# Gathering the part-array products of a windowed-attention kernel into three places per half batch

## The chip, the core and the metric

The kernel runs on one core of one Trainium2 chip. The metric is the device time of one execution in microseconds (us). TensorE does the matrix products, VectorE and ScalarE the element-wise work, GpSimd (POOL) some constants and conversions, and the queues of SyncE and ScalarE start most DMA transfers.

## The reference

```python
def _attn_ref(q, k, v):                       # batch 4, 8 heads, 576 positions, 64 per head
    scores = (1 / np.sqrt(D)) * np.matmul(q, k.transpose(0, 1, 3, 2))
    rel = pos[:, None] - pos[None, :]
    mask_plain = (rel >= 0) & (rel < 32)                          # heads 0 to 3
    mask_dil = (rel >= 0) & (rel < 128) & (rel % 4 == 0)          # heads 4 to 7
    ...
    return np.matmul(attn, v)

def _moe_ref(x, w_in, w_out, alpha):          # 2304 tokens, 512 -> 2048 -> 512
    h = x @ w_in
    g = np.maximum(h, 0.0) + alpha * np.minimum(h, 0.0)
    return g @ w_out

def _moe2_ref(x, w_gate, w1, w2):             # 8 experts, 288 tokens each, 512 -> 1024 -> 512
    logits = x @ w_gate
    ...
    out[mask] = np.maximum(x[mask] @ w1[e], 0.0) @ w2[e]
```

`w_in` and `w_out` come as float64. The softmax goes over the allowed keys; the routing is greedy, highest logit first, until an expert has its 288 tokens. It compares logits, so they have to be exact to float32. The kernel computes the logits from the hidden layer `g` with `we = w_out @ w_gate`, ahead of the second product.

## The kernel before

Phase 1 (up to about 383 us of the profile) makes the attention and the hidden layer. A half batch (`hb`, 0 to 7) is 288 tokens. Its hidden layer is 16 chunks of 128 columns: `hid(hb, f)` is 12 products of the whole array (four parts of the model width, each as high by high, high by low and low by high), 288 columns each. The attention of a half batch is four pairs of heads (`n = 4 hb + pr`; `pr` 0 and 1 are undilated, 2 and 3 dilated).

A pair goes through these steps. `a_t` turns queries and keys (products with the identity), `a_te` takes them out of PSUM. `a_s` makes the scores of a pair: 64 rows of the array per head, so the two heads sit in two opposite quarters (`ps`; five tiles of 96 keys where undilated, four of 72 or 104 keys where dilated). `a_min` (the mask), `a_max`, `a_exp` and `a_norm` are the softmax. `a_pt` turns the weights, `a_pte` takes them out, `a_v` multiplies by the values: two heads side by side in the columns of the array (`po`). `a_vh` and `a_vl` split the result into the high and low part (`xh`, `xl`) that `hid` reads.

The gate logits of a quarter of the chunks are four products side by side, 32 columns of the array each (`logits`, tile `pl`). Half batches 0 to 3 get theirs later (`late`, tile `pll`), from `g` read back out of DRAM by `g_reload`. `l0_rows` turns finished logits into rows (`plt`). The 16 pieces of `w_out` are converted and give `we` by `wg_t`, `wg_m` (four products side by side, 32 columns each, tile `pw`) and `wg_s` (their sum, by a product with `sel`), with `wg_te`, `wg_me` and `wg_se` taking the results out of PSUM.

The order of the instructions is written by hand. Each step is put down with a place by `at(place, step)`; the unit is one chunk (`hid(hb, f)` is at 16 hb + f), and the list is sorted. Every engine works through its own instructions in that order. So the products that use a part of the array stand wherever the table puts them between two chunks: in the kernel before, `a_v` of pair n and `a_s` of pair n + 2 fall between the same two chunks, four times per half batch, and `logits`, `late` and `wg_m` have places of their own.

PSUM has three buffers for `pt`, `po`, `pll` and `plt` (tag `tp`), two for `ph`, one for scores, one for logits and gate weights (tag `lg`). Before chunk 0 the pieces of `w_in` come in over SyncE's queue and are converted by GpSimd, ScalarE and VectorE; the queue also brings queries, keys, values, `alpha` and `w_gate`. Phase 2 (`px`) is the second product with the routing beside it, phase 3 the experts; the change touches neither.

Of the kernel before, what the change touches and what calls it, by code (L numbers as in the profile page):

```python
# [7 lines left out]
F32 = mybir.dt.float32  # L8
# [12 lines left out]
# Places of the steps in the order of issue, in chunks of the hidden layer where they are fractions  # L21
# stages of the attention of a pair, from the first hidden chunk of its time
TA = dict(t=[-2.383, -1.666], te=[-2.203, -1.182], s=-0.544, min=-0.121, max=0.142, exp=[0.933, 2.385], norm=[1.571,
          3.182], pt=[4.914, 6.036], pte=[5.341, 6.32], v=7.254, vh=7.638, vl=7.784, lv=-1.319)
# shifts of the first eight pairs
NB = [2.769, 0.996, 0.321, -0.271, 0.257, 0.621, 0.11, -0.19]
# pairs whose scores get the mask by a product
PM = [0, 1, 2, 3, 4, 5, 6, 7]
# stages of the hidden layer and the gate logits
TH = dict(e=0.253, lg=1.298, lge=2.178, re=-2.126, late=2.001, latee=2.316)  # L30
# half batches whose gate logits come late
LATE = 4
# the late logits: first place, step
TL = [62.259, 2.506]
# pieces of w_in
WB = [-15.49, -15.159, -13.092, -12.092, -10.702, -9.556, -8.948, -5.584, -3.868, -3.649, -2.532, -1.004, -0.811,
      1.134, 3.634, 5.264]
# stages of a piece of w_in
TW = [-0.232, -0.154, 0.786, 1.291, 2.167, 2.365]
# first piece of w_out  # L40
W2 = 8.391
# step of the pieces of w_out
W3 = 3.139
# stages of a piece of w_out
TG = [-1.011, -0.417, 0.749, 1.085, 3.066, 3.243, 4.737, 5.74, 6.781, 6.86]
# end of the attention's buffers, after the last half batch began
TCLOSE = 0.814
# w_out again: loads, first split, step
TO = [-5.329, 3.863, 0.599]
# hidden layer read back: first load, step, first high and low parts  # L50
TGL = [-4.297, 1.335, -1.987, -1.486]
# second product: after which products the last logits and the routing start
XF = [1, 2]
# second product: hidden layer's load, high and low parts, by products modulo 4
GO = [0, 3, 3]
# second product: high and low parts of the first expert's weights
EO = [11, 11]
# time of those on the vector engine, ns
GC = 620
# start of the routing's chain, ns  # L60
RT0 = 3200
# how far it is issued ahead, ns
LEAD = 2000
# PSUM buffers of transposes
TP = 3
# PSUM buffers of long products
# [4 lines left out]
def window_attention_prelu_greedy_moe_kernel(  # L71
# [21 lines left out]
    W = 32                # window, in steps of a head's dilation  # L93
    R = 4                 # dilation of the upper half of the heads
    TQ = 72               # queries of a score tile
    TK = TQ + W           # keys that they can reach
    # undilated heads: queries of a tile (two heads side by side), their step, keys, tiles
    PQ, PS, PK, PT = 64, 56, 96, 5
    HB = S // 2           # tokens of a half batch
# [12 lines left out]
    ra = ctx.enter_context(pool("ra", 4))             # w_in, then experts 0, 2, ..  # L112
    ph_stg, ph_att = ExitStack(), ExitStack()
    stg = ph_stg.enter_context(pool("stg", 2))
    apool = ph_att.enter_context(pool("apool", 2, side="right"))
    ctx.enter_context(tc.manual_schedule())

    w_in, w_out = w_in.bitcast(I32), w_out.bitcast(I32)   # float64 as words (low, high)
# [11 lines left out]
    AT = {}  # L130

    def qk_rows(t, hp):
        # two heads side by side in each row of 128
        return t[:, 2 * hp:2 * hp + 2].rearrange("p h r d -> p (h r d)").rearrange("p (r h d) -> p r h d", r=R, h=2)

    def load_set(hb, s):
# [5 lines left out]
        for t, src in ((qt, q), (kt, k)):  # L142
            off = base + half * HB * D
            if hb == 0:
                # at the start as few transfers as can be
                nc.sync.dma_start(t.rearrange("p h r d -> p h (r d)"),
                                  dram_ap(src, off, [[R * D, TQ], [S * D, 4], [1, R * D]]))
                continue
# [5 lines left out]
    def load_v(hb, s):  # L154
        eng = nc.sync if hb == 0 else nc.scalar
# [3 lines left out]
        if s == 0:  # L159
            # tile t of the half: queries from 56 t, keys from 32 before  # L160
# [22 lines left out]
    # caps of the scores: -1e9 where a key is out of reach  # L183
    BIG = 3.0e38
    NEG = -1.0e9
    capp = apool.tile([P, PK], F32, name="capp", bufs=1)      # undilated: keys from 32 before: 1 <= kcol - q <= 32
    capp0 = apool.tile([P, PT, PK], F32, name="capp0", bufs=1)  # the same, its first tile without keys before 0
    capg = apool.tile([TQ, TK], F32, name="capg", bufs=1)     # dilated: keys from 32 before
    capd = apool.tile([TQ, TQ], F32, name="capd", bufs=1)     # keys from the tile's first: 0 <= q - kcol < 32

    def make_cap(dst, p0, lo, hi):
        # BIG where lo <= kcol - row <= hi, NEG elsewhere
# [14 lines left out]
    # the same caps to be added by a product: 0 in reach, -1e9 out of it  # L207
# [4 lines left out]
    def cap(n):  # L212
        # for a head, or for the two of a pair side by side
# [18 lines left out]
    wg = cpool.tile([P, ND, W], F32, name="wg")  # L232
    nc.gpsimd.memset(wg, 0.0)
# [101 lines left out]
    def wg_se(u):  # L335
        nc.vector.tensor_copy(we[:, u - NU, :], WP.pop(u))
# [889 lines left out]
```

## Time and profile before

| | |
|---|---|
| time, median of 3 runs (lowest to highest) | 863.08 us (863.08 to 863.16) |
| span of the profiled execution, first to last instruction | 859.0 us |
| time outside the span (863.08 - 859.0) | 4.1 us |
| TensorE busy | 823.5 us, 96% of the span |
| VectorE busy | 591.5 us, 69% |
| ScalarE busy | 425.3 us, 50% |

The profile is one execution. Matrix products are pipelined, so the duration of one says less than the distance from one start to the next: below, a block of products is "held" from its own first start to the first start of the next block. A row of a timeline joins equal neighbours (x16 is sixteen records; a float32 product is two records, a transpose one).

### The profile page before, as it was taken

The page shows a single profiled execution, that of the slowest core. Times are in us where ns is not written, and L with a number is a line of the kernel's source. Part 1 is how long each engine was busy: PE and PEld are TensorE (multiplying, and loading weights), DVE is VectorE, ACT ScalarE, POOL GpSimd, SP SyncE. Part 2 cuts the span into 40 slices and gives each one's busy share as a digit, 9 for nine tenths or more (in the row PEclk, how much of TensorE's full clock was granted, in tenths as well). Part 3 has the DMA queues.
Part 4 walks back from the last instruction along what each step waited for, and adds up shares of the span by engine and source line. Part 5 has one row for each costly group of instructions (what it writes and reads, how often), then busy time and mean ns, then how long its engine had stood idle before and what let it go on. Part 6 is the DMA issues. An engine that isn't in the chain of part 4 may idle for free.

```text
span 859.0 us, 17954 instructions
## 1 busy us (share of the span) xinstructions
PE 823.5 (96%) x6827; PEld 730.0 (85%) x6827; DVE 591.5 (69%) x1569; ACT 425.3 (50%) x1210; POOL 91.9 (11%) x138
## 2 busy tenths in 40 slices
PE   5689999999999999999999999999799999999996
PEld 4579999999888888887777777777599999999995
DVE  6899888777656556378888888888654455545630
ACT  4786565867565646482223322322045556555631
POOL 2531010100000000010000000000112212221111
PEclk9999999999999999999999999999889999999998
DMA  8856766654666762566434443334245667665600
GB/s 188 245 173 190 211 205 201 192 173 128 194 174 203 187 175 70 200 200 220 135 85 137 136 135 99 110 103 155 77 123 180 188 189 219 184 185 177 193 28 29
DMA packets 147179, 137.39 MB, mean 160 GB/s; under 512 B 56596, under 2 KB 122004, under 8 KB 147092
## 3 DMA queue, kind: packets, MB, share of 16 engines
q1 hardware_dynamic: 114700, 102.51, 39.8%
q10 hardware_dynamic: 29320, 24.29, 9.6%
q0 software_dynamic: 3072, 9.44, 3.7%
q8 instruction: 54, 0.88, 0.4%
q14 instruction: 33, 0.27, 0.1%
HBM read 103.70 MB, written 32.51 MB: 159 GB/s over the span
## 4 chain that ended last, share of the span: by engine, by line
PE 85%; issue 6%; DMA 3%; DVE 2%; POOL 2%; ACT 1%; SPq 1%; POOLq 0%; ACTq 0%; DVEq 0%
PE ph L124 33%; PE px L124 24%; PE py L124 9%; PE ps L124 3%; PE po L124 3%; PE pc L124 3%; PE pt L485 2%; PE pt L355 2%; PE pll L124 1%; PE pl L124 1%; PE pw L124 1%; POOL out_dram L1130 1%; DMA kt<-in_k_dram 1%; PE pt L316 1%; PE pty L1127 1%
## 5 line engine op out<-in xcount | busy, mean ns | idle before, releaser
L124 PE MATMUL ph<-xh,wih 128*128 128x288 f32 x512 | 161.7, 316 | 0.0
L124 PE MATMUL ph<-xl,wih 128*128 128x288 f32 x512 | 151.5, 296 | 1.2 <-DVE xl L528 1.2
L124 PE MATMUL ph<-xh,wil 128*128 128x288 f32 x512 | 151.1, 295 | 0.0
L124 PE MATMUL px<-woh,gl 128*128 128x512 f32 x288 | 114.7, 398 | 0.0
L124 PE MATMUL px<-woh,gh 128*128 128x512 f32 x288 | 114.7, 398 | 0.0
L124 PE MATMUL px<-wol,gh 128*128 128x512 f32 x288 | 114.4, 397 | 0.0
L556 DVE SCALAR_TENSOR_TENSOR g<-gt,nal,gt 128x288 f32<-128x288 f32 x104 | 54.6, 527 | 81.6 <-ACT gt L555 67.5
L124 PEld LDWEIGHTS ph<-xh,wih 128*128 128x128 f32 x512 | 96.7, 189 | 8.4 <-issue 3.3
L624 ACT ACTIVATE gh<-gl 128x512 fp32r<-128x512 f32 x72 | 45.4, 633 | 116.2 <-DMA gl<-gD 59.3
L124 PEld LDWEIGHTS ph<-xl,wih 128*128 128x128 f32 x512 | 96.9, 189 | 1.5 <-DVE xl L528 1.5
L124 PEld LDWEIGHTS ph<-xh,wil 128*128 128x128 f32 x512 | 96.6, 189 | 0.0
L554 ACT ACTIVATE gt<-ph 128x288 f32<-128x288 f32 x104 | 42.6, 410 | 93.0 <-PE ph L124 87.9
L124 PE MATMUL ph<-xeh,w1h 128*128 128x288 f32 x256 | 78.5, 307 | 0.6 <-ACT xeh L1170 0.6
L124 PE MATMUL py<-hh,w2h 128*128 128x288 f32 x256 | 77.9, 304 | 0.0
L124 PE MATMUL ph<-xel,w1h 128*128 128x288 f32 x256 | 76.8, 300 | 0.0
L124 PE MATMUL ph<-xeh,w1l 128*128 128x288 f32 x256 | 76.5, 299 | 0.0
L124 PE MATMUL py<-hh,w2l 128*128 128x288 f32 x256 | 76.0, 297 | 0.0
L124 PE MATMUL py<-hl,w2h 128*128 128x288 f32 x256 | 75.3, 294 | 0.0
L1047 DVE TENSOR_TENSOR w2l<-wraw,w2h 128x512 fp32r<-128x512 f32 x64 | 43.2, 684 | 28.9 <-ACT w2h L1045 28.9
L124 PEld LDWEIGHTS px<-woh,gh 128*128 128x128 f32 x288 | 54.4, 189 | 10.1 <-issue 0.5
L124 PEld LDWEIGHTS px<-woh,gl 128*128 128x128 f32 x288 | 54.3, 189 | 9.8
L124 PEld LDWEIGHTS px<-wol,gh 128*128 128x128 f32 x288 | 54.3, 189 | 9.7
(229 smaller groups left out, 1798.4 us busy)
## 6 DMA issues: line engine op xcount, KB each, us to landing
wraw<-in_moe_w_dram SPq DMA_DIRECT2D x64, 512.0 KB
gD<-g SPq DMA_DIRECT2D x32, 576.0 KB
gl<-gD SPq DMA_DIRECT2D x72, 256.0 KB
g<-gD ACTq DMA_DIRECT2D x16, 576.0 KB
raw<-in_moe_w_in_dram SPq DMA_DIRECT2D x16, 512.0 KB
raw<-in_moe_w_out_dram SPq DMA_DIRECT2D x16, 512.0 KB
x2D<-xo ACTq DMA_DIRECT2D x18, 256.0 KB
woD<-sg SPq DMA_DIRECT2D x16, 256.0 KB
```

The source lines that it names most:

```text
L124: nc.tensor.matmul(o, l, r, start=start, stop=stop, **kw)
L316: nc.tensor.transpose(pt[:, d, :], WV[u][:, d * P:(d + 1) * P], ident)
L355: nc.tensor.transpose(pt[:, r, :], qk_rows(t, hp)[:, r].rearrange("p h d -> p (h d)"), ident[:TQ, :TQ])
L485: nc.tensor.transpose(pt[:w, t, :], sm[:, h, t, :] if s else sm[:, i.start + t, :], ident[:c, :c])
L554: nc.scalar.activation(t, ph, AF.Relu, scale=-1.0)
L556: nc.vector.scalar_tensor_tensor(g[:, f % 4, :], t, nal[:, f:f + 1], t2, op0=ALU.mult, op1=ALU.add)
L624: nc.scalar.activation(GQ[i][0], GQ[i][1].bitcast(F32), AF.Copy)
L1047: V.tensor_tensor(lo, t, hi.bitcast(F32), op=ALU.subtract)
L1127: nc.tensor.transpose(pt[:, d, :], YT[e][:, d, 96 * t:96 * (t + 1)], ident)
L1130: st = nc.gpsimd.indirect_dma_start(out=out, out_offset=bass.IndirectOffsetOnAxis(ap=idx[:, t, e:e + 1], axis=0), in_=yo[:, t, :], in_offs ...
```

## The change

From half batch 2 on, the products on parts of the array go to three places ("visits") per half batch, taken from a table `VIS`. The first visit has the undilated scores of both pairs, the second and third the scores of one dilated pair each; the value products of the half batch before, the gate logits and the late logits are put beside them (two late groups as one step that accumulates in one PSUM buffer, from a pool of four buffers of its own, `cv2`). The undilated scores of two pairs become one step: five tiles, each with four products in the four quarters of the array, in two PSUM banks; the second pair has its heads crossed, which `a_v` undoes. `wg_m` becomes four accumulating products on the whole array with the turned piece of `w_out` as the stationary operand and 8 columns of `w_gate` streamed; `wg_s` and `wg_se` are gone. The values of half batch 0 are loaded over ScalarE's queue; `alpha` and `w_gate` get places of their own in SyncE's queue (-9.629 and -1.172). All the tables of places are new. Most of the remaining lines of the diff remove comments.

```diff
-TA = dict(t=[-2.383, -1.666], te=[-2.203, -1.182], s=-0.544, min=-0.121, max=0.142, exp=[0.933, 2.385], norm=[1.571,
-          3.182], pt=[4.914, 6.036], pte=[5.341, 6.32], v=7.254, vh=7.638, vl=7.784, lv=-1.319)
...
+VIS = {2: [-20.691, -15.75, -9.6], 3: [-22.405, -16.792, -10.341]}
+NS = {2: [0.872, 3.895, 7.108, 11.086], 3: [0.065, 3.656, 8.081, 12.2]}
+NT = [[-6.44, -7.011], [-3.296, -1.965], [1.891, 3.55], [7.565, 8.76]]
...
+TB = dict(min=-0.298, max=0.426, exp=[1.413, 2.426], norm=[1.511, 3.832], pt=[4.869, 5.964], pte=[4.877, 5.951])
+TV = [[0.4, 0.55], [0.65, 0.95], [0.4, 0.657], [0.325, 0.656]]
...
     def load_v(hb, s):
-        eng = nc.sync if hb == 0 else nc.scalar
+        eng = nc.scalar
...
     def wg_m(u):
-        pw = WP[u] = psum.tile([P, P], F32, name="pw", tag="lg", bufs=1)
+        pw = WP[u] = psum.tile([P, E], F32, name="pw", tag="lg", bufs=1)
+        wt = WV.pop(u)
         for d in range(ND):
-            mm(pw[W * d:W * (d + 1), :], wg[:, d, :], WV[u][:, d, :], True, True, tile_position=(0, W * d))
+            mm(pw, wt[:, d, :], wg[:, d, :], d == 0, d == ND - 1)
...
     def a_s(n):
...
+        if s == 0 and hb > 1:
+
+            ps = psum.tile([P, 2, 512], F32, name="ps", tag="sc", bufs=1)[:, :, :PT * PK]
+            ps = ps.rearrange("p i (t k) -> p i t k", k=PK)
+            for t in range(PT):
+                k0 = half * HB + PS * t
+                for i in range(2):
+                    for h in range(2):
+                        o = D * (h if i == 0 else 1 - h)
+                        mm(ps[o:o + D, i, t, :], ST[n + i][D * h:D * (h + 1), PS * t:PS * t + PQ],
+                           KT[pr + i][D * h:D * (h + 1), k0:k0 + PK], True, True)
+            for i in range(2):
+                ST[n + i] = ps[:, i], [ps[:, i]], PK
+            return
...
     def late(hb, fq):
+
         pl = psum.tile([P, HB], F32, name="pll", tag="tp", bufs=TP)
-        g = G.pop((hb, fq))
-        for i in range(4):
-            mm(pl[W * i:W * (i + 1), :], we[:, 4 * fq + i, :], g[:, i, :], True, True, tile_position=(0, W * i))
+        for j in range(2):
+            g = G.pop((hb, fq + j))
+            for i in range(4):
+                mm(pl[W * i:W * (i + 1), :], we[:, 4 * (fq + j) + i, :], g[:, i, :], j == 0, j == 1,
+                   tile_position=(0, W * i))
...
+    for hb in range(2, NHB):
+        vis = [NF * hb + x for x in VIS[min(hb, 3)]]
+        after = [NF * (hb + 1) + x for x in VIS[3]]
...
+            x = vis[(0, 0, 1, 2)[pr]]
+            if pr != 1:
+                at(x + 0.04, a_s, n)
...
+            x = (vis[2], vis[2], after[0], after[1])[pr]
+            at(x, a_v, n)
+            at(x + TV[pr][0], a_vh, n)
+            at(x + TV[pr][1], a_vl, n)
...
+            t0 = NF * hb + 4 * fq + 4.7
+            t = min([x for x in visits if x >= t0] + [t0 + (4.9 - 0.2, 0.9, 2.5, 0)[fq]])
+            if (hb, fq) != (NHB - 1, 3):
+                at(t + 0.02, logits, hb, fq)
...
-            nc.sync.dma_start(al, alpha.rearrange("(f p) -> p f", p=P))
-            nc.sync.dma_start(wg[:, :, :E], w_gate.rearrange("(d p) e -> p d e", p=P))
+    at(TS[0], nc.sync.dma_start, al, alpha.rearrange("(f p) -> p f", p=P))
+    at(TS[1], nc.sync.dma_start, wg, w_gate.rearrange("(d p) e -> p d e", p=P))
```

## Rows read from the trace of the kernel before

**Rows 1.** The page: span; busy time, share and instructions of each engine.

```profile
span 859.0 us, 17954 instructions
PE 823.5 (96%) x6827; PEld 730.0 (85%) x6827; DVE 591.5 (69%) x1569; ACT 425.3 (50%) x1210; POOL 91.9 (11%) x138
```

**Rows 2.** Busy time by stretch: us, engines in turn, clock, DMA share, GB/s.

```profile
27.00:52.00 25.00, 18.76 (x184) 14.91 (x183) 24.66 (x50) 21.83 (x75) 10.29 (x9) 1.00 0.82 227
52.00:96.00 44.00, 42.59 (x438) 39.04 (x437) 41.44 (x97) 29.93 (x100) 8.87 (x12) 1.00 0.63 176
...
139.00:223.00 84.00, 84.00 (x916) 78.27 (x915) 61.60 (x157) 61.02 (x217) 5.38 (x9) 1.00 0.62 182
223.00:312.00 89.00, 89.00 (x952) 75.37 (x954) 53.20 (x137) 49.44 (x192) 0.42 (x3) 1.00 0.67 186
```

**Rows 3.** Timeline, TensorE, a chunk alone: start us, us, engine, line, op, tiles.

```profile
359.44 0.30 PE L124 MATMUL ph<-xh,wih 128*128 128x288 f32 x1
...
361.04 0.30 PE L124 MATMUL ph<-xh,wih 128*128 128x288 f32 x1
```

**Rows 4.** Timeline, TensorE, around one stop: values, then undilated scores.

```profile
254.21 0.29 PE L124 MATMUL ph<-xh,wil 128*128 128x288 f32 x1
254.43 0.72 PE L124 MATMUL po<-aT,vt 104*64 104x72 f32 x16
255.08 1.04 PE L124 MATMUL ps<-kT,qT 64*64 64x96 f32 x20
256.06 0.40 PE L124 MATMUL ph<-xh,wih 128*128 128x288 f32 x1
256.29 0.30 PE L124 MATMUL ph<-xl,wih 128*128 128x288 f32 x1
```

**Rows 5.** Timeline, TensorE, gate logits alone and two groups in a row.

```profile
251.78 0.69 PE L124 MATMUL pll<-g,we 128*32 128x288 f32 x8
252.40 0.47 PE L355 MATMUL pt<-ident,kt 72*128 72x72 f32 x4
...
257.85 0.69 PE L124 MATMUL pl<-g,we 128*32 128x288 f32 x8
258.36 0.67 PE L124 MATMUL pll<-g,we 128*32 128x288 f32 x8
```

**Rows 6.** Timeline, TensorE, gate weights, and logits turned into rows.

```profile
110.53 0.30 PE L124 MATMUL pw<-sel,wu 128*128 128x32 f32 x2
110.67 0.45 PE L355 MATMUL pt<-ident,qt 72*128 72x72 f32 x4
...
113.16 0.42 PE L124 MATMUL pw<-wt,wg 128*32 128x128 f32 x8
113.52 0.40 PE L124 MATMUL ph<-xh,wih 128*128 128x288 f32 x1
...
274.52 1.18 PE L124 MATMUL plt<-sel,lgS 128*128 128x8 f32 x10
275.56 0.45 PE L355 MATMUL pt<-ident,kt 72*128 72x72 f32 x4
```

**Rows 7.** Timeline, SyncE's queue at the start.

```profile
14.27 3.89 SPq L722 DMA_DIRECT2D wg<-in_moe_w_gate_dram  x1
18.20 1.93 SPq L254 DMA_DIRECT2D raw<-in_moe_w_in_dram  x4
```

**Rows 8.** Timeline, VectorE, at the start and before the first chunk ends.

```profile
23.44 0.69 DVE L287 SCALAR_TENSOR_TENSOR mag<-raw,tlow 128x512 int32<-128x512 int32 x1 [3.22 <-POOL tlow L280]
...
53.33 0.77 DVE L473 TENSOR_SCALAR st<-st 128x2 f32<-128x2 f32 x1
...
54.99 0.45 DVE L528 TENSOR_TENSOR xl<-po,xh 128x288 fp32r<-128x288 f32 x1
```

**Rows 9.** VectorE groups, 139 to 375 us: busy us, mean ns, idle before.

```profile
L439 DVE TENSOR_TENSOR sm<-ps,capg 72x832 f32<-72x832 f32 x6 | 6.1, 1014 | 0.0
L589 DVE TENSOR_TENSOR lgS<-lgS,pll 128x288 f32<-128x288 f32 x12 | 5.4, 447 | 0.2
```

## What the change was predicted to do

> **What bounds the kernel now.** I read the page first: TensorE is busy for 96% of the span, so the question is where it works and where it waits [rows 1]. The table by stretches answers that. From 139 to 312 us TensorE is busy in every microsecond, at the full granted clock, while VectorE has work for 61.6 of 84 and 53.2 of 89 us [rows 2]. There the time is the sum of what TensorE's blocks hold it, and whatever VectorE or ScalarE does is hidden as long as it is not late. Before 96 us it is different: from 27 to 52 us VectorE is busy 24.7 of 25 us and TensorE 18.8; from 52 to 96 us both are nearly full [rows 2]. The change lies in these stretches; phases 2 and 3 keep their instructions, and nothing in them is tied to an absolute time, so what phase 1 gains the end gains.
>
> The third view is TensorE's timeline, read by the distance between starts. A chunk of the hidden layer with nothing beside it holds 1.60 us, 0.133 per product [rows 3]. Around a stop (a run of products on parts of the array) that distance grows: the last product ahead of one is followed after 0.22 instead of 0.13, and the first product behind one is held 0.23 [rows 4]. So a stop costs its neighbours 0.09 and 0.10 beyond its own products. Inside, too, a change of shape has a price: a group of gate logits holds 0.62 before other work and 0.51 before its like, a tail of 0.11 [rows 5].
>
> **The change, part by part.** Sorting the places that the tables give (from chunk 0 on) gives the counts; the rows give the prices.
>
> *Fewer stops.* Before there are 68 stops, after it 29: 20 visits, 4 of the unchanged pairs of half batch 1, and 5 of logits that found no visit in time. Chunks that follow a stop go from 38 to 19, chunks that precede one from 52 to 25; transposes that stand beside one go from 47 to 13. Chunks: 19 x 0.10 + 27 x 0.09 = 4.3 us, less 0.3 because 4 more of them now follow transposes, which also cost an entry (estimate 0.07). For the 34 transposes I take 0.065 each, between nothing and a chunk's 0.10: 2.2. Together -6.3 (from -4.0 to -7.4).
>
> *Scores in four quarters.* 12 blocks of undilated scores at 0.98 [rows 4] become 6. The price of the new block is not in the trace. Two rounds of 288 columns hold 0.51 [rows 5], so a round of 96 columns is 0.085; the old block has 20 records, and ten rounds plus the tail make 0.85 + 0.11 = 0.96, about the 0.98 seen. So two quarters do work side by side. The new block has 40 records. With four side by side it is ten rounds again, 0.99 with a few nanoseconds for the starts, and no less, since each quarter streams as many columns as before. With two it is twenty rounds: 1.70 + 0.11 = 1.81. I take 0.99, by the nearest row: gate logits run four abreast (8 records of 288 columns in two rounds) [rows 5]. 12 x 0.98 - 6 x 0.99 = -5.8, at worst -0.9.
>
> The Trainium skill has two rules against this. In "TensorEngine Tiling (Array Packing)", Gotcha 1, different row tiles cannot use the same PSUM bank at the same time. The trace differs: both heads of a pair write one bank from different row halves, and 0.98 is the time of two abreast, where one at a time would be 1.81 [rows 4]. In "TensorE: Matmul & The Clock Gate", Part 3 (what overlaps), a weight load overlaps running products only where the row group differs. The trace differs again: the value block has its two heads in the same rows, and its 16 records of 72 columns hold 0.65 [rows 4], eight rounds of 0.064 plus a tail, where sixteen would be 1.13. No row shows two row halves in the same columns. By either rule the new block would be 1.81, the second rival below.
>
> *Late logits.* 16 groups at 0.62 become 8 steps of two groups; seven are followed by a group of their kind and hold about 1.00, one 1.11: 9.9 becomes 8.1, -1.8. *Value products.* In six visits two value blocks of one shape stand together and save a tail: 6 x 0.11 = -0.7.
>
> *Gate weights.* Before, 0.36 for the four narrow products and 0.14 for their sum, 0.50 per piece [rows 6]. The four full products are 8 records with 128 columns of stationary operand and 8 streamed. The nearest row has that very shape: `plt`, 10 records in 1.04 [rows 6], so 0.83. The lower bound is the sum with `sel`, also 128 columns of stationary operand: 0.07 a record, 0.57. I take 0.83: 16 x 0.33 = +5.3 us (at least +1.1). This part costs TensorE more than it saves. What it saves is one eviction per piece on VectorE, which is hidden.
>
> TensorE's sum: -6.3 - 5.8 - 1.8 - 0.7 + 5.3 = -9.3 us.
>
> *New waits.* At a visit the new scores are masked by VectorE (place +0.4) ahead of `a_vl` (+0.55) and `late_e` (+0.56), which free the PSUM that the next transposes ask for. Behind the last score of a visit with a dilated pair VectorE needs up to 1.01 for the mask [rows 9], 0.45 for `xl` [rows 8] and 0.45 for the logits [rows 9], 1.91; TensorE has one chunk meanwhile, 1.60 + 0.10 for its entry. The rest, some 0.2 us, is a wait; queued behind the waiting transpose are the next chunk and then ScalarE's evictions. This is in six visits. With the first chunk of a half batch, which needs `xl` of the last pair, I take +1.0 in all, from 0 to +3. Loads of queries, keys and values are issued 6 to 12 chunks ahead, as before. `g_reload`'s transfers stay on ScalarE's queue, 16 before and after, a visit ahead.
>
> *The start.* Three things move. First, the order on VectorE: the first chunk waits for `xl` of pair 3, and ahead of it stands the normalisation of pair 4, from 53.33 to 54.99 [rows 8]. The new places put it behind: up to -1.7, but VectorE is full and owes the same work to the next chunks, so I take -1.2. Second, SyncE's queue: the issue of `w_gate` lasts 3.89 us and piece 3 of `w_in` goes out behind it at 18.20 [rows 7]; VectorE waits 3.22 us for that piece [rows 8]. With values, `alpha` and `w_gate` out of the way piece 3 leaves earlier, up to -3.2. Against that, the values now compete on a second queue with the first queries and keys, so I take -1.5. Third, half batch 2 begins earlier, which brings a mask, a maximum and a copy of keys (some 1.5 us, an estimate from the like of [rows 9]) into the full stretch before chunk 16; I take +0.2. The start: -2.5, from -5 to +1.5.
>
> Sum: -9.3 + 1.0 - 2.5 = -10.8 us. The span goes from 859.0 to 848.2. The median of the runs is 863.08, 4.1 above the span, and that part stays: 852.3.
>
> **The rivals.** *Quarters two by two.* The block of four quarters holds 1.81: 6 x 0.82 = 4.9 us more, 857.2. For it: no row shows two row halves in the same columns, and the two rules above. Against it: what two halves, two columns and four columns do.
>
> *The start gains nothing.* Queries and keys of half batch 2 (`load_set(2, 0)`) go from place 3.5 to -1.9 and there wait in SyncE's queue for the transposes of pair 5 (-0.8). Behind them, with `w_gate`'s 3.89 us, stand the last two pieces of `w_in`, whose signs ScalarE asks for at places 3.1 and 4.9, ahead of its evictions. If those come late, the start is at +1 instead of -2.5: 855.8.
>
> *Full products are cheaper.* If 8 records hold 0.57, the sum is 4.2 lower: 848.1.
>
> *Slower: visits that wait for VectorE.* Each visit takes all three `tp` buffers. If the transposes behind it are given the buffer whose `a_vl` stands behind the next chunk's eviction (the second value block's is at +0.95), TensorE waits for VectorE's whole chain, about 1.9 us, not for its rest. Six such visits eat 11.4 us and the gain is gone; two per half batch, 12 visits, cost 22.9: 875. Against it: the first value block's buffer and the late logits' are both given up before the transposes' places (+0.64), so one should be free.
>
> **How the numbers follow.** The forecast, 852.3, has a chance of 55% (its own range 849 to 855); quarters two by two 18%; no gain at the start 13%; cheap full products 7%; the waiting visits 7%. The range from 848 to 858.5 holds the forecast, both dearer cases and about half of the cheap one, and leaves out the waiting visits and the tails, under 2 in 10. A measurement of this kernel can tell some 0.2%, 1.7 us, from no change. All cases but the waiting visits are faster by more than that; part of those, and a mix of two dear ones, come out within it: faster 0.88, same 0.05, slower 0.07.
>
> **What would show it.** In the profile after: TensorE busy throughout from chunk 16 to the end of phase 1, and that stretch 8 to 9 us shorter (before: `hid(1, 0)` to the first `px`); `ps` blocks of 40 records held 0.99, not 1.81; `pw` blocks of 8 records held 0.83; three stops per half batch; no `wg` issue ahead of the raw pieces; the first chunk's wait for `xl` gone or shorter. I am wrong if TensorE shows waits for `xl` or the logits' copies above 0.3 us a visit, or if VectorE, emptied of nothing at the start, keeps the first chunks where they were.

## The result, and the profile after

The changed kernel takes 849.98 us in the median, against 863.08 for the kernel before: a ratio of 0.9853, 95% interval 0.9836 to 0.9870. The forecast was 852.3 us, in a range from 848 to 858.5. The profiled execution has a span of 846.7 us and took 848.51.

The page of the kernel after, first its span and the busy time of each engine, then the table by stretches (us, then busy time and instructions of each engine in turn, clock, DMA share, GB/s), to be read against [rows 1, 2]:

```profile
span 846.7 us, 17836 instructions
PE 813.8 (96%) x6795; PEld 733.6 (87%) x6795; DVE 583.1 (69%) x1545; ACT 422.3 (50%) x1210; POOL 90.0 (11%) x138
...
27.00:52.00 25.00, 18.22 (x169) 15.03 (x170) 23.87 (x48) 20.88 (x70) 7.45 (x8) 1.00 0.82 213
52.00:96.00 44.00, 42.76 (x440) 39.34 (x440) 39.74 (x93) 30.18 (x104) 8.71 (x12) 1.00 0.69 194
134.00:215.00 81.00, 81.00 (x886) 79.20 (x885) 58.77 (x148) 59.45 (x214) 6.99 (x11) 1.00 0.58 173
215.00:300.00 85.00, 85.00 (x958) 77.51 (x958) 52.04 (x135) 48.89 (x196) 0.30 (x1) 1.00 0.69 195
```

TensorE's share is the same 96%, of a shorter span: of the 12.3 us that the span is shorter, 9.7 are busy time (823.5 to 813.8), so it mostly works less. From 134 to 300 us it is busy in every microsecond, as before, and the view of TensorE's waits has no entry from 90 to 375 us. A visit on its timeline (start us, us, engine, line, op, tiles), one of the dear kind:

```profile
245.49 0.72 PE L149 MATMUL po<-aT,vt 104*64 104x72 f32 x16
246.15 1.18 PE L149 MATMUL pll<-g,we 128*32 128x288 f32 x16
247.14 0.67 PE L149 MATMUL pl<-g,we 128*32 128x288 f32 x8
247.74 1.06 PE L149 MATMUL ps<-kT,qT 64*64 64x96 f32 x40
248.72 0.40 PE L149 MATMUL ph<-xh,wih 128*128 128x288 f32 x1
```

By the distance between starts: values 0.66, two late groups of logits 0.99, one early group 0.60, and 40 records of undilated scores 0.98, where 20 held the same before [rows 4].

Where the time went is read from four marks on TensorE's timeline: the first product of chunk `hid(1, 0)`, the first `px` (phase 2 begins), the first `pj` (phase 2 nearly over) and the end of the span. The first and the second mark in the kernel before, then in the changed kernel:

```profile
95.94 0.40 PE L124 MATMUL ph<-xh,wih 128*128 128x288 f32 x1
...
382.66 0.40 PE L124 MATMUL px<-woh,gh 128*128 128x512 f32 x1
```

```profile
95.53 0.40 PE L149 MATMUL ph<-xh,wih 128*128 128x288 f32 x1
...
372.83 0.50 PE L149 MATMUL px<-woh,gh 128*128 128x512 f32 x1
```

All kernels of this study in one table, in us; the distances are worked out from the marks.

| kernel | hid(1,0) | to px | px to pj | pj to end | span | median of the runs |
|---|---|---|---|---|---|---|
| before | 95.94 | 286.72 | 233.35 | 242.99 | 859.0 | 863.08 |
| after | 95.53 | 277.30 | 231.92 | 241.95 | 846.7 | 849.98 |
| after_again | 96.02 | 277.59 | 231.92 | 242.87 | 848.4 | 850.04 |
| a1_values_sync | 94.83 | 277.89 | 231.88 | 243.20 | 847.8 | 848.22 |
| a2_two_by_two | 96.53 | 280.06 | 231.92 | 241.89 | 850.4 | 853.20 |
| a3_narrow_weights | 96.36 | 277.69 | 233.91 | 241.94 | 849.9 | 851.59 |
| a4_steps_apart | 95.75 | 281.44 | 232.68 | 242.13 | 852.0 | 854.09 |
| a5_joined | 93.53 | 277.95 | 233.99 | 242.83 | 848.3 | 849.78 |
| a6_one_bank | 93.97 | 275.67 | 232.33 | 242.63 | 844.6 | 846.55 |
| a7_early_reads | 93.50 | 277.75 | 232.36 | 242.49 | 846.1 | 848.24 |
| b1_full_products | 97.91 | 289.75 | 232.96 | 242.48 | 863.1 | 864.96 |
| b2_logits_last | 99.25 | 286.68 | 234.14 | 243.03 | 863.1 | 862.97 |
| b3_early_reads | 99.66 | 286.72 | 232.87 | 242.25 | 861.5 | 862.09 |
| b4_start_seam | 94.95 | 286.68 | 232.28 | 242.09 | 856.0 | 858.64 |

Of the 12.3 us between the two spans the stretch of attention beside the hidden layer has 9.4, the start 0.4, phase 2 1.4 and the rest 1.0. The column from `pj` to the end shows that the last figure is chance: no kernel here differs there, and the profiles scatter over 1.3 us. The first column shows chance of another kind, to which we come at the start's runs.

### The profile page after: what moved, and what is told of

Read it like the earlier page. It is cut to its first block, busy times and chain, and to the rows that moved or that the text cites. A ratio compares the mean times of both kernels' runs of the same rounds, so it can differ in the third digit from the quotient of the medians.

```text
span 846.7 us, 17836 instructions
## 1 busy us (share of the span) xinstructions
PE 813.8 (96%) x6795; PEld 733.6 (87%) x6795; DVE 583.1 (69%) x1545; ACT 422.3 (50%) x1210; POOL 90.0 (11%) x138
## 4 chain that ended last, share of the span: by engine, by line
PE 85%; issue 6%; DVE 2%; DMA 2%; ACT 2%; POOL 1%; SPq 0%; ACTq 0%; POOLq 0%
PE ph L149 33%; PE px L149 24%; PE py L149 9%; PE ps L149 3%; PE pc L149 3%; PE po L149 2%; PE pt L517 2%; PE pw L149 2%; PE pt L373 1%; PE pll L149 1%; PE pl L149 1%; POOL out_dram L1218 1%; PE pt L341 1%; DMA vt<-in_v_dram 1%; DVE wil L336 1%
```

## The experiments

Names with a are variants of the changed kernel, with b of the kernel before. Their medians come with runs of the kernel before on the same chip: 862.76 us beside after_again, a1, a2 and a3, 862.09 beside a4, a5, b1 and b2, 862.81 beside a6, a7 and b3, 862.52 beside b4.

**The changed kernel again.**

> The changed kernel once more, as the neighbour of the three that follow. Expected 848.5 to 851.7 us, the width of its first four times; if it is one level with noise of its own, the same two clusters near 848.6 and 851.5 show again, while the kernel before stays within 1 us.

Measured: 850.04 us (848.76 to 851.75), 0.9857 of before (0.9835 to 0.9879), spread evenly over its 3 us. The two clusters were chance; the kernel before spread more widely still, 858.6 to 865.7, where the expectation had it within 1 us. So differences of under a microsecond are read from the marks, not from medians.

**Are the four quarters the source?** The order of the twenty products of a step:

```diff
-            for t in range(PT):
-                k0 = half * HB + PS * t
-                for i in range(2):
+            for i in range(2):
+                for t in range(PT):
+                    k0 = half * HB + PS * t
                     for h in range(2):
```

> The changed kernel with the undilated scores' 20 products of a step in another order: the ten of one pair, then the ten of the other; every product writes where it did. Theory (four products that lie on different quarters run beside each other, two only as two): a step of 20 takes 1.81 us instead of 0.99, 6 steps, so 4.9 us slower, 854 to 855.5 us. Rival (it is the cheaper surroundings of a step, not the quarters, that made it short): a step stays near 1.0 us and the time within 0.5 us of the changed kernel beside it.

Measured: 853.20 us, 3.2 more than its neighbour. TensorE's timeline of this variant, the same visit as above:

```profile
250.37 1.60 PE L149 MATMUL ps<-kT,qT 64*64 64x96 f32 x40
251.90 0.40 PE L149 MATMUL ph<-xh,wih 128*128 128x288 f32 x1
```

A step holds 1.53 us instead of 0.98, and six steps make 3.3: the theory in kind, with a smaller size. The starts of the single records, which the timeline above puts in one line, say why it is not 1.81. In the changed kernel products start in fours, 0.007 us apart, every 0.083 us. Here they start in twos every 0.083 us, but in each of the six steps the fifteenth record is the second pair's first (it has the wait for that pair's operands): it starts when six of the first pair's twenty have not started yet. Its quarters are free, and it comes 0.32 us earlier than a round behind the first pair's last would, which covers the distance from 1.81 to 1.53. So even this order has the quarters overlap. What tells four from two is the order in which the instructions stand.

**Is the gathering worth it?** Logits put one or two chunks behind the visit that they rode on:

```diff
+                t += (2.0 if t < t0 + 5 else 1.0) if t in visits else 0.0
                 at(t + 0.02, logits, hb, fq)
...
-        at(t + 0.01, late, hb, fq)
+        at(t + 1.01, late, hb, fq)
```

> The changed kernel with the gathering undone for the gate logits: the logits of hidden layers read back stand one chunk behind the visit that they were part of, the others one or two chunks behind it. The same products, 12 more stops with products of narrow tiles. Theory (a step beside another narrow step saves about 0.09 us on the chunk ahead, 0.10 on the chunk behind or 0.03 to 0.1 on transposes, and 0.4 for logits right behind others of their shape): from the first chunk of half batch 1 to the first px 2.0 to 4.5 us longer, the time up to 852 to 854 us. Rival (only the products' own places count, the neighbours cost the same anywhere): within 0.5 us in that stretch.

Measured: 854.09 us, and 281.44 in the stretch, 4.1 over the changed kernel. It is made of two things. The view of TensorE's waits from 90 to 380 us (us in total, times, longest):

```profile
PE pll L149 <- ACT qT L397: 1.8, 2, 0.9
```

The late logits take a buffer of the transposes, and off the visit it is not free. The other 2.3 us are shapes beside other shapes: held times of transposes up 3.0 in all (which holds a part of what the waits delay), of chunks 0.3, of late logits 0.7. The timeline has twelve more stops than the changed kernel's (41 against 29), so some 0.2 us each.

**Gate weights: full or narrow products?** Three runs. First the old form in the changed kernel:

```diff
-            mm(pw, wt[:, d, :], wg[:, d, :], d == 0, d == ND - 1)
+            mm(pw[W * d:W * (d + 1), :], wg[:, d, :], WV[u][:, d, :], True, True, tile_position=(0, W * d))
...
+        mm(pw, WV.pop(u), sel, True, True)
```

> The changed kernel with the gate weights seen from the hidden layer made as in the kernel before: four narrow products side by side, and one product with the selecting columns a chunk later. By the terms of the prediction the products cost 16 x (0.50 - 0.83) = -5.3 us, and the 14 more stops with products some 0.16 us each, +2.2: 3 us faster than the changed kernel beside it, 845.5 to 848 us. Rival (a stop costs what the narrow products save): within 0.7 us of the changed kernel. Second rival (VectorE's 32 more instructions end up ahead of the chunks' own): slower by 1 us or more.

Measured: 851.59 us, 1.5 more than its neighbour, where 3 less was expected; the stretch is the same to 0.1 us. The `pw` blocks give back 4.9 us (12.83 to 7.91), the chunks lose 2.9 and the transposes 2.4. Some of that is a wait. The timeline of the variant (in brackets the idle time and what ended it):

```profile
163.17 0.30 PE L149 MATMUL pw<-sel,wu 128*128 128x32 f32 x2
...
166.09 0.43 PE L149 MATMUL pw<-wt,wg 128*32 128x128 f32 x8 [0.94 <-DVE we L361]
```

One chunk lies between a piece's second product and the next piece's first; both use the one `lg` buffer, and VectorE comes late with the copy. Three such waits make 2.2 us. Without them some 3 us (2.9 + 2.4 - 2.2) are left around the steps; the expectations of the next runs, written before this was sorted out, have it as 2.2 around the stops and 3 of waits. The timeline has 24 more places at which a step of the gate weights stands apart from other part-array products, not 14: ten with the narrow products and 14 with a sum alone, so some 0.13 us each. The 1.5 us by which the median is higher are not in this stretch: phase 2 takes 2.0 longer (233.91, see the seam).

Then the new form in the kernel before, alone (the diff the other way round):

> The kernel before with one part of the change alone: the gate weights by four full products of 8 columns each, no second product and no copy between. The prediction's step: +5.3 us for the products, -1.8 us for 11 stops fewer, so 3.5 us slower than the kernel before. What the run of the changed kernel with narrow products showed meanwhile: the products themselves 4.9 us, and 2.2 us around them that fall away because a full product leaves the chunks and transposes beside it alone; +2.7 us. Rival (what falls away around them pays for them wholly): within 0.7 us of the kernel before.

Measured: 864.96 us, ratio 1.0031 (1.0018 to 1.0043), 2.9 us slower; the stretch is 3.0 longer, 289.75. `pw` costs 4.7 more (8.14 to 12.81), chunks and transposes give back 0.7 and 0.9. So in its old surroundings this part of the change loses time, and it does not pay for itself in any run here.

Where the give-back comes from is seen in the rows of either form: the distance from a chunk's last product to the block behind it. Changed kernel (a full product ahead of values, then one ahead of a chunk), then the variant a6 below:

```profile
163.88 0.29 PE L149 MATMUL ph<-xh,wil 128*128 128x288 f32 x1
164.02 0.95 PE L149 MATMUL pw<-wg,wt 128*128 128x8 f32 x8
164.90 0.47 PE L149 MATMUL po<-aT,vt 104*64 104x72 f32 x8
```

```profile
130.51 1.00 PE L149 MATMUL pw<-wg,wt 128*128 128x8 f32 x8
131.37 0.38 PE L149 MATMUL ph<-xh,wih 128*128 128x288 f32 x1
131.59 0.29 PE L149 MATMUL ph<-xl,wih 128*128 128x288 f32 x1
```

```profile
154.00 0.29 PE L149 MATMUL ph<-xh,wil 128*128 128x288 f32 x1
154.22 0.43 PE L149 MATMUL pw<-wt,wg 128*32 128x128 f32 x8
154.58 0.41 PE L149 MATMUL pw<-sel,wu 128*128 128x32 f32 x2
154.82 0.45 PE L381 MATMUL pt<-ident,qt 72*128 72x72 f32 x4
```

Ahead of a full product the chunk ends as if another chunk followed, 0.14; ahead of a narrow one it pays 0.22. Behind a full product there is little to gain: the next chunk's first product is held 0.22 there, 0.24 behind narrow ones and 0.13 within a chunk. Where a full product stands ahead of a narrow block it pays for the change of shape itself: it holds 0.88 ahead of values, 0.86 ahead of chunks and 0.81 ahead of transposes. The Trainium skill, "TensorEngine Tiling (Array Packing)", Key Properties, has the rule: changing the tiling mode, not just the tile, drains the engine. The trace agrees, and prices it: 0.08 us here, 0.22 against 0.14 at a chunk's end.

**A narrow form that doesn't wait.** The first try took a buffer of the transposes for the second product and put it at the next piece's stop; both also have the values of half batch 0 on SyncE (next heading), and the second the early reads of the seam (the heading after it).

> A version meant to beat both: the changed kernel with the values of half batch 0 on SyncE's queue and with narrow products for the gate weights, where the second product of a piece of w_out stands right in front of the first product of the next piece, in a PSUM buffer of the transposes, so that there are as many stops as in the changed kernel. The run with a stop of its own for each showed 4.9 us less in the products, 2.2 us more around them and some 3 us of new waits for VectorE's copies. Theory: no wait now, and 1 to 2.2 us around the 16 stops: 2.7 to 3.9 us faster than the version with the values on SyncE alone, 844.3 to 845.5 us. Rival (the copies on VectorE come late here too, and TensorE waits at the shared buffer): a wait for we or wu in the trace, and 847 to 849 us.

Measured: 849.78 us, slower than even the rival's range, and by another way: no wait for `we` or `wu`, but waits of 1.3 us at `pt` and 0.6 at `pw`, ended by ScalarE's `qT`, the price of one more user of the transposes' buffers, and 0.8 at the last logits, where phase 2 takes 233.99 (see the seam). The second try takes columns of the same buffer:

```diff
+        pw = WP[u] = psum.tile([P, P + W], F32, name="pw", tag="lg", bufs=1)
+                mm(pw[W * d:W * (d + 1), :P], wg[:, d, :], WV[u][:, d, :], True, True, tile_position=(0, W * d))
+            mm(pw[:, P:], WV.pop((u - 1, "s")), sel, True, True)
```

> The former with narrow products for the gate weights, the second product of a piece of w_out at the same stop as the next piece's first ones and in columns of the same PSUM buffer, so that neither waits for a copy of the other nor takes a buffer of the transposes. Theory (a narrow step costs its 0.36 + 0.14 us and what it adds around it, 1 to 2.2 us over the 16 stops, and the earlier two versions lost their gain to waits alone): from the first chunk of half batch 1 to the first px 274 to 275.5 us instead of 277.3 to 277.9, the time 2.2 to 3.5 us below the version with the early reads alone, 844 to 846 us. Rival (narrow products cost as much around them as full products cost themselves, waits or none): 277 us or more in that stretch, and the same time as the version with the early reads alone.

Measured: 846.55 us (845.07 to 848.27), 0.9819 of before (0.9804 to 0.9835), the fastest of all, 1.7 under the version with the early reads alone. The stretch is 275.67, 2.1 under that version's; both are just short of the ranges given. `pw` costs 3.3 us less (12.84 to 9.53; ten records hold 0.60), chunks and transposes together 1.5 more, and there is no wait. The narrow form is the better one here, by two thirds of what its products save.

**The start.** The values of half batch 0 back on SyncE's queue:

```diff
-        eng = nc.scalar
+        eng = nc.sync if hb == 0 else nc.scalar
```

> The changed kernel with the values of half batch 0 back on SyncE's queue; alpha and the gate weights stay at their new places. In the trace of the changed kernel the queries and keys (0,1) are issued at 4.56 and 8.48 us where the kernel before issues them at 2.09 and 2.52, with the transfer of the values in their way. Theory (the values on ScalarE's queue hold SyncE's transfers up, and that is why the start gained 0.4 us and not 2.5): the raw pieces 1 and 2 and the keys are back at their times of before, the first chunk of half batch 1 starts 1 to 2.5 us earlier, 847.3 to 849 us against about 850 of the changed kernel beside it. Rival (the start is bound by the conversion of the pieces on GpSimd and VectorE, not by the loads): within 0.4 us of the changed kernel. Second rival (six more issues on SyncE delay the raw pieces): 0.5 to 1.5 us slower.

Measured: 848.22 us (847.85 to 849.64), 1.8 less than its neighbour; `hid(1, 0)` starts 1.2 us earlier, and in the three later variants with this line 2.1 to 2.5 earlier than in after_again. Two views show what stood in the way. SyncE's queue in the changed kernel, the queries and keys (0, 1) issued at 4.56 and 8.48 us (2.07 and 2.50 in this variant):

```profile
1.62 0.57 SPq L278 DMA_DIRECT2D raw<-in_moe_w_in_dram  x1
4.56 0.30 SPq L171 DMA_DIRECT2D qt<-in_q_dram  x1
8.48 0.30 SPq L171 DMA_DIRECT2D kt<-in_k_dram  x1
```

And GpSimd's first conversions, of the kernel before, the changed kernel and the last variant of this study, b4, in turn:

```profile
12.96 0.78 POOL L280 TENSOR_SCALAR tlow<-raw 128x512 uint16<-128x512 uint32 x1 [4.06 <-DMA raw<-in_moe_w_in_dram]
...
22.63 0.77 POOL L280 TENSOR_SCALAR tlow<-raw 128x512 uint16<-128x512 uint32 x1 [6.81 <-DMA raw<-in_moe_w_in_dram]
23.48 1.43 POOL L227 TENSOR_SCALAR capm<-capd 72x288 bf16<-72x288 f32 x1
```

```profile
15.60 0.77 POOL L305 TENSOR_SCALAR tlow<-raw 128x512 uint16<-128x512 uint32 x1 [5.96 <-DMA raw<-in_moe_w_in_dram]
```

```profile
12.42 0.77 POOL L280 TENSOR_SCALAR tlow<-raw 128x512 uint16<-128x512 uint32 x1 [3.86 <-DMA raw<-in_moe_w_in_dram]
...
19.75 0.78 POOL L280 TENSOR_SCALAR tlow<-raw 128x512 uint16<-128x512 uint32 x1 [4.47 <-DMA raw<-in_moe_w_in_dram]
20.60 1.43 POOL L227 TENSOR_SCALAR capm<-capd 72x288 bf16<-72x288 f32 x1
```

The second piece is converted 2.6 us later in the changed kernel than before, since the values come in beside it: with them back on SyncE's queue it is at 12.72 (a1). The fourth is what [rows 7] showed: before, it left behind `w_gate`. It delays not only VectorE but the mask `capm`, which stands behind it on GpSimd and for which TensorE's `ps` waits 7.0 us; without `w_gate` in the way (b4) the mask is 2.9 us earlier and TensorE waits 4.5.

**The seam between phase 1 and phase 2.** Phase 2 was 1.4 us shorter after, which the prediction had not forecast. In the kernel before the last logits hold two lines:

```profile
383.45 0.69 PE L124 MATMUL pl<-g,we 128*32 128x288 f32 x6
384.63 0.67 PE L124 MATMUL pl<-g,we 128*32 128x288 f32 x2 [0.49 <-DVE g L556]
```

ScalarE stood at `gh` for the read-back `gl` ahead of the last chunk's activations; the row is the first below, and of b2 the second:

```profile
382.79 0.63 ACT L624 ACTIVATE gh<-gl 128x512 fp32r<-128x512 f32 x1 [0.81 <-DMA gl<-gD]
```

```profile
386.74 0.63 ACT L624 ACTIVATE gh<-gl 128x512 fp32r<-128x512 f32 x1 [2.15 <-DMA gl<-gD]
```

The change moves the logits of the third quarter to the seam. That alone in the kernel before:

```diff
-                        at(t + TH["lg"], logits, hb, f // 4)
+                        at(t + (4.2 if t == NF * NHB - 5 else TH["lg"]), logits, hb, f // 4)
```

> The kernel before with one step moved: the logits of the third quarter of the last half batch stand between its last chunk and the first product of phase 2, as in the changed kernel, instead of two chunks from the end. Theory (they fill the time in which the last logits wait for VectorE's g, which stood behind a read-back of the hidden layer): the last logits are held 0.62 us instead of 1.78, and the stretch from the first px to pj is 1.2 to 1.5 us shorter; the time 0.8 to 1.5 us shorter. Rival (the read-back's landing sets it, and that changes from kernel to kernel): the last logits are held over 1.2 us still, and the time is the same within 0.4 us.

Measured: 862.97 us, ratio 1.0004 (0.9993 to 1.0016). The last logits are held 2.36 us: the rival. ScalarE waits 2.15 us for the read instead of 0.81, and that takes all that the cover gave. Then the reads alone, the first four issued together ahead of a store that waits for VectorE:

```diff
-        at(NF * NHB - 1 + TGL[0] + i * TGL[1], g_load, i)
+        at(NF * NHB - 1 + TGL[0] + (0.01 * i if i < 4 else i * TGL[1]), g_load, i)
```

> The kernel before with one thing moved: the read-back of the hidden layer's first four pieces (gl) is issued together, ahead of the store of the last half batch's third quarter, so that the second to fourth no longer stand behind that store on SyncE's queue, which waits for VectorE's g. Theory (the wait at the last logits, 1.16 us in the kernel before and 1.6 to 2 us in two of the runs so far, is ScalarE standing at gh for that read-back, ahead of the last chunk's activations): no wait of the last logits for g, they are held 0.62 us, and the stretch from the first px to pj is 1.2 to 2.2 us shorter than 233.4 to 234.2. Rival (the wait has another source, or the reads take transfers from the weights that are read beside them): still held over 1 us, the stretch over 233 us.

Measured: 862.09 us, ratio 0.9991 (0.9982 to 1.0000). `gh` waits for no read any more, but the logits are held 1.32: what is left is the time that the last chunk's own activations take, with nothing in between to cover it. Both are needed, the cover and the early read. In the changed kernel too:

> The changed kernel with the values of half batch 0 on SyncE's queue and the same early read-back. Where the second piece was read in 3.8 to 4.2 us in the changed kernel there was no wait to remove in its profile; but its runs lie up to 3 us apart. Theory (some executions have that wait of up to 2 us, others not): the profile as without the early reads, the median 0 to 1 us lower and the runs closer together, 847.2 to 848.5 us. Rival: no difference, 848.2 us with the same width.

Measured: 848.24 us (847.71 to 850.07) against 848.22 for a1: no difference, as the rival had it; the changed kernel's read happened to be in time. In a3 and a5 it was not, and phase 2 took 233.9 and 234.0. Why the same read takes 4 us in one kernel and 6 in another wasn't settled.

**Start and seam in the kernel before.** Three moves: both of the seam, and the loads of `alpha` and `w_gate` behind the raw pieces.

```diff
-            nc.sync.dma_start(al, alpha.rearrange("(f p) -> p f", p=P))
-            nc.sync.dma_start(wg[:, :, :E], w_gate.rearrange("(d p) e -> p d e", p=P))
+    at(-9.629, nc.sync.dma_start, al, alpha.rearrange("(f p) -> p f", p=P))
+    at(-1.172, nc.sync.dma_start, wg[:, :, :E], w_gate.rearrange("(d p) e -> p d e", p=P))
```

> The kernel before with three small moves that lie far apart in time, so that the trace keeps them apart: alpha and the gate weights' loads go behind the raw pieces on SyncE's queue, as in the changed kernel; the logits of the last half batch's third quarter stand behind its last chunk; and the read-back's first four pieces are issued ahead of the store. Each of the last two alone left the last logits held 2.36 and 1.32 us. Theory for the end of phase 1: with both they are held 0.62 us, and from the first px to pj it takes 231.9 to 232.4 us (before 233.4, and 232.9 to 234.1 in the three variants of it). Rival: still over 1 us. Theory for the start: in the kernel before and two kernels with the same start the first chunk of half batch 1 began at 95.9, 99.3 and 99.7 us, in the changed kernel and three with its start at 95.5 to 96.5; if the gate weights in the way of piece 3 are what costs the 2.2 us between the means, it begins at 95 to 97 us here. Rival (the order on VectorE did it): at 97.5 to 99.7 us. Both theories together: 1.2 to 3.5 us faster than the kernel before, 859.5 to 861.5 us.

Measured: 858.64 us, ratio 0.9961 (0.9946 to 0.9976), 3.9 us faster, a little more than expected. The last logits:

```profile
381.01 0.69 PE L124 MATMUL pl<-g,we 128*32 128x288 f32 x8
...
382.53 0.69 PE L124 MATMUL pl<-g,we 128*32 128x288 f32 x8
383.15 0.50 PE L124 MATMUL px<-woh,gh 128*128 128x512 f32 x1
```

They hold 0.62 and phase 2 takes 232.28. The start is at 94.95. Two kernels with the start of the kernel before, and b1 with nearly that, had 97.9 to 99.7; so the place of `w_gate` (and `alpha`) alone is worth 1 us against the luckiest profile, that of the kernel before, and 3.3 against the mean of the three with the same start (98.3). Steadier marks say the same: the very first chunk starts at 47.89 here, and at 50.85 to 51.59 in the four profiles with `w_gate` at its old place; and the medians' 3.9 us less 1.1 of the seam leave 2.8. VectorE's order was not touched.

## Why the prediction was right, point by point

*TensorE's sum, -9.3.* Measured -9.4 from `hid(1, 0)` to the first `px`, where the prediction's signs gave 8 to 9, and its terms by the held times of all blocks between the two marks: chunks 191.48 to 187.69 and transposes 29.54 to 26.80, together -6.5 (forecast for the stops -6.3); scores 18.96 to 14.17, -4.8 in the stretch, and 1.0 more for the sixth step, which lies ahead of it (-5.8); late logits 9.89 to 7.95, -1.9 (-1.8); values 16.59 to 15.70, -0.9 (-0.7); gate weights 8.14 to 12.83, +4.7 (+5.3, of which 15 of 16 pieces lie in the stretch). Every term is within 0.6 us. That the two sums agree to 0.1 is partly luck: the forecast counts from chunk 0 on, and without the sixth step of scores and the first piece of gate weights, which lie ahead of `hid(1, 0)`, it is some -8.7 for this stretch.

*What the stops were.* The size was right, and so were the counts: TensorE's timeline has 68 before and 29 after. Not all of it is gathering. Of the 39 stops that fell away 13 are steps of gate weights (b1, which changes these alone, has 55), which the prediction counted but did not name; its paragraph on the gate weights gives their new form no saving on TensorE. b1 shows that 1.6 us come from there (a6 1.5, a3 some 3). Gathering the logits is worth some 2.3 us around them, and keeps 1.8 us of waits away (a4). The rest, some 2.6 us, is left to scores and values standing together, which no run took apart.

*Quarters.* 0.98 as forecast. The rival's price was wrong: two by two is 1.53, not 1.81, because the second pair starts before the first has ended (a2): by the starts of the records, with six records of the first still to start. The Trainium skill's two rules that spoke against it ("TensorEngine Tiling (Array Packing)", Gotcha 1, and "TensorE: Matmul & The Clock Gate", Part 3) are not borne out by this block, in which two row halves write the same bank in the same round, and two products on the same rows, in different columns, start 0.014 us apart.

*New waits, +1.0.* None came. The visits' buffers were free in time; with logits a chunk later, or one more user of the buffers, waits of 1.8 and 1.9 us do come (a4, a5). The mechanism is there, and the changed places keep clear of it.

*The start, -2.5.* Two profiles say -0.4. But the kernel before had a lucky profile: with the same start b2 and b3 reach `hid(1, 0)` at 99.3 and 99.7 instead of 95.9, while five kernels with the changed start lie between 95.5 and 96.5. Between the means (98.3 and 96.0) it is -2.2. These are means of three and of five profiles that scatter by 3.7 and 1.0 us, so that -2.2 comes near -2.5 is partly luck. Of the causes named, `w_gate` in the way is shown (b4). "The values compete on a second queue" has the right sign; the prediction left 1.7 us for it (3.2 less 1.5), and a1 and the three later variants show 1.2 to 2.5. The order of `xl` and the normalisation was not tried alone, but its sign came. What the first chunk waited for, before and after:

```profile
PE ph L124 <- DVE xl L528: 1.2, 1, 1.2
```

```profile
PE ph L149 <- ACT xh L557: 0.9, 1, 0.9
```

With the old order the wait for `xl` is 1.2 to 1.9 us in four profiles, and 2.7 in b4, where the chunk starts earlier; in the changed kernel and its repetition 0.9 and 1.1, and `xh` ends it.

*Outside the span.* The step that failed: 4.1 us were carried over as time outside the span. In all 13 profiled executions with a time beside their span the difference is 1.7 to 1.9 (848.51 - 846.7). The execution profiled of before must therefore have taken some 860.8 us (estimate, 859.0 + 1.8), 2.3 under its median, and its start lies 2.3 ahead of the mean of the three. Against the median the account is -9.4 for TensorE, -2.2 for the start, -1.4 for the seam: -13.0, and 863.08 - 849.98 = 13.1 (12.7 where both ran again on one chip, so the agreement to 0.1 is luck too).

*Phase 2 and 3 unchanged.* Their instructions are; the seam into phase 2 is not, and the prediction didn't look at what waits where a step lands. It is worth 1.4 us.

So the forecast was 2.3 us high: 1.0 for waits that didn't come and 1.4 for the seam. The time outside the span did no harm in the end: a difference laid on the median needs no such term, and against the median the start did gain what was forecast.

## What to carry to other kernels

Count a step on parts of the array by its neighbours too: here a step of narrow products that stood apart cost TensorE some 0.2 us around it, so steps are worth gathering. A full-width product that costs more by itself got a third of that back in place (1.6 of 4.7 us, b1) and the narrow form without waits was still better (a6); only a run of each form in its place tells. Products that touch different quarters overlap only as far as the instruction order lets them, so interleave them by quarter. Before a gain at the start of a kernel is read from one profile, compare that profile's own time with the median: the difference may lie exactly there.

## What was not expected of the hardware

The start scatters. With the same instructions `hid(1, 0)` began at 95.9, 99.3 and 99.7 us. Part of it is TensorE's clock: in b3 the granted clock is still 0.50 (of the two levels the lower, 1.2 GHz) from 50 to 62 us, and 0.97 behind.

```profile
50.00:58.00 8.00, 5.94 (x37) 4.71 (x37) 7.59 (x15) 5.02 (x13) 6.60 (x4) 0.50 0.65 206
58.00:62.00 4.00, 4.00 (x28) 3.78 (x24) 2.52 (x5) 2.31 (x8) 0.77 (x1) 0.50 0.01 4
62.00:70.00 8.00, 8.00 (x85) 7.25 (x85) 7.28 (x16) 5.66 (x15) 1.18 (x1) 0.97 0.35 103
```

The products of the first two chunks of the hidden layer held 5.30 and 3.05 us there, 4.34 and 1.70 in the profile of before. Where no change of the clock was recorded ahead, the column gives 1.00, as from 27 us on in [rows 2] and in the table after; the products tell more. In the first chunk they start 0.24 us apart in every profile of this study, as at b3's 0.50, and 0.13 apart at full clock [rows 3]. The profile of before has 0.13 from its second chunk (57.1 us) on, b2 and b3 have 0.24 there still (58.5 and 59.2 us) and 0.13 from the third. Part is also the first chunk's wait for `xl`, 1.2 us in the profile of before and 1.9 in those two. What makes the clock rise earlier in one execution than in another is open.

Products also overtake each other within TensorE: in a2 a product on a free quarter started while six records that stand ahead of it in the order of the instructions had not started yet, in all six steps.
